# One load for w_down, fewer pieces at the end, and an output row cast in two halves: a cached attention block with a feed-forward block beside it, on one core

## The chip, the core and the metric

The kernel runs on one core of one Trainium2 chip. The metric is the device time of one execution in microseconds (us). The kernel before took 2534.58 us, the median of 3 runs (2534.54 to 2534.76). One further execution was profiled; it took 2534.51 us, of which the profile's span, from the first instruction to the last, covers 2532.6 us. All numbers taken from views of the profile belong to that execution.

## The reference

One token `x` (512 values) goes through two blocks, and a gate mixes the results.

```
g = sigmoid((x * gate_w).sum())
q = x @ wq                                  # 32 heads of 128
p = softmax(q . k_cache * 128 ** -0.5)      # 65536 keys for each head
a = (p @ v_cache) @ wo                      # wo is 4096 x 512
b = (silu(x @ w_gate) * (x @ w_up)) @ w_down   # 512 -> 1792 -> 512
out = g * a + (1 - g) * b                   # 512 values, bf16
```

`k_cache` and `v_cache` have the shape 1 x 32 x 65536 x 128 in bf16, 512 MB each. Every byte of them is used once, with a single query. `w_down` is 1792 x 512, 1.75 MB.

## The kernel before

**Tiles.** K and V come in tiles of 4 MB: 128 partitions, on each 128 cache rows of 128 values, so 32 KB that lie together in DRAM. There are N = 128 tiles of each, four to a head (`G`). All large tiles share one pool, `ring`, of five buffers of 4 MB: wq, the K and V tiles, the gate and up weights (`gu_t`), w_down (`wd_t`), and the last 16 heads of wo (`wo_t`).

**Scores.** `products` (L230) lets VectorE multiply a K tile by the query, in place (L240), and fold 128 columns to 16 by three additions of halves (L244). `scores` (L249) sums the 16 columns on TensorE into `S_ps`. After a head's four tiles `row_max` and `exponentials` (L263, L273) form the weights, with a maximum over all partitions taken through TensorE.

**Values.** `values` (L296) runs 32 matmuls for a V tile (L302), each with four cache rows of each partition, into a 4 x 512 accumulator `O_ps`, so that a head's result lies on the four diagonal blocks. `head_copy` (L311) brings it to SBUF on ScalarE; for the last head ScalarE takes one half and VectorE the other. `head_column` (L320) turns the four blocks into a column with eight small TensorE passes into `oh_ps`, and ScalarE scales it into `oT`. `project` (L334) adds the head's product with wo to the row `a_ps`. Heads 0 to 15 are projected as they come; heads 16 to 31 (`WH` = 16) only at the very end, when `wo_t` has been loaded.

**The order of work** is written out by hand: the pools run under a manual schedule, and the list `steps` (L344) says for each step which K tile and which V tile are treated. V starts four tiles behind K and is held back to eight tiles behind; after the last K tile, eight V tiles remain. In each step the loads are issued first, all of them from SyncE and so on one DMA queue, in the order in which they stand in the code. A load waits for its buffer to come free. It also waits for its completion semaphore: SyncE's loads go around eight of them, so a load waits until the one eight before it has landed. SyncE takes its instructions in order, so one load that waits holds those behind it.

**w_down before.** It is laid on 64 partitions, 28 rows of 512 on each (28 KB). `load_wd` (L142) loads it in eight transfers of eight partitions (L146): two before the third K tile (L150), six after it (L359). To fit that layout `feed_forward_mid` (L189) brings the hidden vector from 128 x 14 to 64 x 28 by two matmuls (L202) and a copy on ScalarE (L206), then runs 28 matmuls (L209) into `b_ps`.

**The end before.** The last V tile comes in five pieces, of 32, 32, 32, 16 and 16 of the 128 cache rows of each partition (L365); behind it come the last 16 heads of wo in five pieces of 4, 4, 4, 2 and 2 heads (L157, L366). After the last matmul of `values` the code projects heads 16 to 19, then forms the last head's column, then projects heads 20 to 31 (L405 to L410). VectorE casts the row of 512 (L413), and SyncE stores it (L414).

Of the kernel before, what the change touches and what calls it, by code (L numbers as in the profile page):

```python
# [8 lines left out]
ACT = mybir.ActivationFunctionType  # L9
ALU = mybir.AluOpType  # L10
AXIS = mybir.AxisListType
P = 128
# [3 lines left out]
NB = 128  # L16
# [9 lines left out]
def kernel(  # L26
# [14 lines left out]
    nc = tc.nc  # L41
    bf16 = mybir.dt.bfloat16
    f32 = mybir.dt.float32

    _, H, Sk, Dh = A_k_cache.shape
    D = A_x.shape[2]
    F = B_w_gate.shape[1]
    KT = D // P
    FT = F // P
    G = Sk // (NB * P)  # L50
    NBH = Sk // P
    N = H * G
# [4 lines left out]
    consts = ctx.enter_context(tc.tile_pool(name="consts", bufs=1))  # L57
# [7 lines left out]
    psum_m = ctx.enter_context(tc.tile_pool(name="psum_m", bufs=2, space=bass.MemoryType.PSUM))  # L65
# [3 lines left out]
    def big(name):  # L69
        return ring.tile([P, NB * Dh], bf16, name=name, tag="big")  # L70
# [12 lines left out]
    ident_b = consts.tile([P, P], bf16, name="ident_b")  # L83
# [14 lines left out]
    a_ps = psum_a.tile([1, D], f32, name="a_ps")  # L98

    K_tiles, V_tiles, S_tiles, P_tiles, O_tiles = {}, {}, {}, {}, {}  # L100

    def load(dst, cache, n, name, cuts=(0, NB)):
        h, g = divmod(n, G)
        t = big(name)
        view = t.rearrange("p (j d) -> p j d", d=Dh)
        src = cache[0, h, g * NB * P : (g + 1) * NB * P, :].rearrange("(p j) d -> p j d", j=NB)
        for a, b in zip(cuts[:-1], cuts[1:]):
            nc.sync.dma_start(out=view[:, a:b, :], in_=src[:, a:b, :])
        dst[n] = view
# [24 lines left out]
    nc.sync.dma_start(out=wgu_sb[:, 0], in_=B_w_gate.rearrange("(p t) f -> p t f", t=KT))  # L134
    nc.sync.dma_start(out=wgu_sb[:, 1], in_=B_w_up.rearrange("(p t) f -> p t f", t=KT))
    wd_t = big("wd_t")
    HP = P // 2
    GT = F // HP
    wd_sb = wd_t[:HP, : GT * D].rearrange("p (t n) -> p t n", t=GT)
    wd_rows = B_w_down.rearrange("(p t) n -> p t n", t=GT)  # L140

    def load_wd(*which):  # L142
        for i in which:
            lo = (0, 1, 2, 3, 32, 33, 34, 35)[i]
            part = slice(lo, lo + 29, 4)
            nc.sync.dma_start(out=wd_sb[part], in_=wd_rows[part])  # L146

    with nc.allow_non_contiguous_dma(reason="small"):
        nc.sync.dma_start(out=gwT, in_=gate_w.rearrange("(p t) -> p t", t=KT))
    load_wd(0, 1)  # L150
    WG = 4
    wo_tiles = {}

    WH = H // 2
    wo_end = []

    def load_wo_end(cuts):  # L157
        t = big("wo_t")[:, : (H - WH) * D].rearrange("p (h n) -> p h n", n=D)
        rows = A_wo[WH * P :, :].rearrange("(h p) n -> p h n", p=P)
        for a, b in zip(cuts[:-1], cuts[1:]):  # L160
            nc.sync.dma_start(out=t[:, a:b, :], in_=rows[:, a:b, :])
        wo_end.append(t)

    def load_wo(g):
        wo_tiles[g] = wo_pool.tile([P, WG, D], bf16, name="wo_sb")
        rows = A_wo[g * WG * P : (g + 1) * WG * P, :]
        nc.sync.dma_start(out=wo_tiles[g], in_=rows.rearrange("(h p) n -> p h n", p=P))
# [21 lines left out]
    def feed_forward_mid(gu_sb, eg):  # L189
        nc.vector.tensor_scalar_add(eg, eg, 1.0)  # L190
        nc.vector.reciprocal(eg, eg)
        hprod = consts.tile([P, FT], f32, name="hprod")
        nc.vector.tensor_tensor(out=hprod, in0=gu_sb[:, :FT], in1=eg, op=ALU.mult)
        hT = consts.tile([P, FT], bf16, name="hT")
        nc.vector.tensor_tensor(out=hT, in0=hprod, in1=gu_sb[:, FT:], op=ALU.mult)
        xg = consts.tile([P, KT], f32, name="xg")
        nc.vector.tensor_tensor(out=xg, in0=xT, in1=gwT, op=ALU.mult)
        xs = consts.tile([P, 1], f32, name="xs")
        nc.vector.tensor_reduce(out=xs, in_=xg, axis=AXIS.X, op=ALU.add)
        h_ps = psum_m.tile([HP, GT], f32, name="h_ps", tag="misc")  # L200
        for r in range(2):
            nc.tensor.matmul(  # L202
                h_ps[:, r * FT : (r + 1) * FT], lhsT=ident_b[:, r::2], rhs=hT, start=True, stop=True
            )
        h2 = consts.tile([HP, GT], bf16, name="h2")
        nc.scalar.activation(out=h2, in_=h_ps, func=ACT.Copy)  # L206
        b_ps = psum_m.tile([1, D], f32, name="b_ps", tag="misc")
        for t in range(GT):
            nc.tensor.matmul(  # L209
                b_ps, lhsT=h2[:, t : t + 1], rhs=wd_sb[:, t, :], start=(t == 0), stop=(t == GT - 1)  # L210
            )
        g_ps = psum_m.tile([P, 1], f32, name="g_ps", tag="misc")
        nc.tensor.matmul(g_ps, lhsT=ones_f, rhs=xs, start=True, stop=True)
        eg2 = consts.tile([P, 1], f32, name="eg2")
        nc.scalar.activation(out=eg2, in_=g_ps, func=ACT.Exp, scale=-1.0)
        return b_ps, eg2
# [13 lines left out]
    def products(n, a=0, b=NB):  # L230

        h = n // G
        K = K_tiles[n][:, a:b, :]
        qb = q_bc[:, h * Dh : (h + 1) * Dh]
        q_rep = bass.AP(
            tensor=qb.tensor,
            offset=qb.offset,
            ap=[list(qb.ap[0]), [0, b - a], [1, Dh]],
        )
        yield nc.vector.tensor_tensor(out=K, in0=K, in1=q_rep, op=ALU.mult)  # L240
        half = Dh
        while half > WIDTH:
            half //= 2
            yield nc.vector.tensor_tensor(  # L244
                out=K[:, :, 0:half], in0=K[:, :, 0:half], in1=K[:, :, half : 2 * half],
                op=ALU.add,
            )
# [43 lines left out]
    def weight(h, tot_ps):  # L291
        recip = small.tile([P, 1], f32, name="recip")
        nc.vector.reciprocal(recip, tot_ps)  # L293
        nc.vector.tensor_tensor(out=rg[:, h : h + 1], in0=recip, in1=gval, op=ALU.mult)
# [39 lines left out]
    def project(h):  # L334
        nc.tensor.matmul(  # L335
            a_ps,
            lhsT=oT[:, h : h + 1],
            rhs=wo_tiles[h // WG][:, h % WG, :] if h < WH else wo_end[0][:, h - WH, :],
            start=False,
            stop=(h == H - 1),  # L340
        )
# [3 lines left out]
    v = 0  # L345
# [9 lines left out]
    for n, v in steps:  # L355
        if n is not None and n > 1:
            load(K_tiles, A_k_cache, n, "K_t")
        if n == 2:
            load_wd(2, 3, 4, 5, 6, 7)  # L359
        if n == 3:  # L360
            load_wo(0)
        if v is not None:
            if v % (WG * G) == 2 * G and v // (WG * G) + 1 < WH // WG:
                load_wo(v // (WG * G) + 1)
            load(V_tiles, A_v_cache, v, "V_t", (0, NB) if v < N - 2 else (0, 64, NB) if v < N - 1 else (0, 32, 64, 96, 112, NB))  # L365
            if v == N - 1:  # L366
                load_wo_end((0, 4, 8, 12, 14, 16))
        if n == 2:
            ff = feed_forward_mid(*ff)
        halves = (0, NB // 2)  # L370
        vector = iter(()) if n is None else products(n)
        if n == 0:
            vector = (i for a in halves for i in products(n, a, a + NB // 2))
        top_of = None
        if n is None:
            top_of = H - 1 if S_tiles else None
        elif n % G == 0 and n > 0:
            top_of = n // G - 1
            vector = (i for a in halves for i in products(n, a, a + NB // 2))
        if top_of is not None:  # L380
            next(vector, None)
            mT_ps = row_max(top_of)
            next(vector, None)
            exponentials(top_of, mT_ps)
        for _ in vector:
            pass
        if n == 1:
            ff = feed_forward_in()
        if n == 3:
            feed_forward_out(*ff)  # L390
        if tot_ps is not None:
            weight(*tot_ps)
            tot_ps = None
        if done is not None:
            head_column(done, head_copy(done))
        if v is not None:
            values(v)
        if top_of is not None:
            tot_ps = top_of, total(top_of)
        if n is not None:  # L400
            scores(n)
        if done is not None and done < WH:
            project(done)
        done = v // G if v is not None and v % G == G - 1 else None
    O_last = head_copy(H - 1, last=True)  # L405
    for h in range(WH, WH + 4):
        project(h)
    head_column(H - 1, O_last)
    for h in range(WH + 4, H):
        project(h)  # L410

    out_sb = consts.tile([1, D], bf16, name="out_sb")
    nc.vector.tensor_copy(out=out_sb, in_=a_ps)  # L413
    nc.sync.dma_start(out=out[0], in_=out_sb)  # L414


# [28 lines left out]
```

## Time and profile before

| What | Value | Where it is read |
|---|---|---|
| profiled execution | 2534.51 us | times |
| its span | 2532.6 us | head of the page |
| three other runs | median 2534.58 us, 2534.54 to 2534.76 | times |
| bytes read from DRAM | 1087.64 MB, 429 GB/s over the span | page, part 3 |
| VectorE busy | 2175.5 us, 86% of the span | page, part 1 |
| TensorE matmuls busy | 1742.4 us, 69% | page, part 1 |
| share of the end's chain: DMA, PE, DVE | 68%, 22%, 10% | page, part 4 |
| matmul of `values`, 128 x 512 | 4096 of 453 ns busy | page, part 5 |
| matmul with w_down, 64 x 512 | 28, 12.1 us busy in all | page, part 5 |
| wo's last heads, pieces of 512 KB and 256 KB | 3 and 2 | view of the DMA issues, last 83 us |

PE is TensorE, PEld its weight loads, DVE is VectorE, ACT is ScalarE, SP is SyncE (SPq its DMA issues). The chain of part 4 is followed back from the last instruction, at each step to whatever released it. A group's line gives its source line, engine, operation, output and input, then busy time, mean length and the idle time ahead of it with what ended it. Matmuls overlap, so a group's busy time is more than the time by which it moves the end. The stage views give, for a stretch of time, each engine's busy time, then the granted TensorE clock (1.00 is full speed), then the mean busy share of the 16 DMA engines and their rate.

### The profile page before, as it was taken

Reading aid. Unit: us, or ns where it says so; the run is one execution under the profiler, and the core shown is the slowest. Engines: PE = TensorE matmul, PEld = TensorE weight load, DVE = VectorE, ACT = ScalarE, POOL = GpSimd, SP = SyncE. Lnnn points to the kernel's source line nnn. Section 1 sums busy time; section 2 is a strip of 40 time slices with the busy share of each in tenths; the row PEclk is TensorE's granted clock in tenths of the full one; section 3 lists DMA queues with packets and bytes.
Section 4 is the critical chain, followed back from the end, with each engine's and each line's share of the span. In section 5 each row is a group of like instructions: output and inputs, shape, how many; then the busy total and the mean of one; then the engine's idle time right before and its main releaser. Section 6 shows DMA issues by size and latency. Waiting matters only on the chain.

```text
span 2532.6 us, 15260 instructions
## 1 busy us (share of the span) xinstructions
PE 1742.4 (69%) x6738; PEld 712.1 (28%) x6738; DVE 2175.5 (86%) x784; ACT 75.9 (3%) x207; POOL 0.7 (0%) x6
## 2 busy tenths in 40 slices
PE   4677666776677666676776677667666776677679
PEld 2222222222222222222222223222222232222223
DVE  7998888888888999998888888888888888888860
ACT  1000000000000000000000000000000000000000
POOL 0000000000000000000000000000000000000000
PEclk7677777777777676677777777777777777777779
DMA  9999999999999999999999999999999999999998
GB/s 415 433 433 430 433 433 433 432 430 435 432 432 434 431 433 432 432 433 433 432 434 433 432 434 433 432 432 434 432 431 434 433 430 434 434 431 433 434 432 339
DMA packets 42884, 1088.63 MB, mean 430 GB/s; under 512 B 4737, under 2 KB 8834, under 8 KB 9090
## 3 DMA queue, kind: packets, MB, share of 16 engines
q1 hardware_dynamic: 42674, 1087.66, 99.7%
q8 instruction: 53, 0.87, 0.1%
q14 instruction: 13, 0.11, 0.0%
q10 hardware_dynamic: 144, 0.00, 0.0%
HBM read 1087.64 MB, written 0.00 MB: 429 GB/s over the span
## 4 chain that ended last, share of the span: by engine, by line
DMA 68%; PE 22%; DVE 10%; issue 1%; ACT 0%; DVEq 0%; SPq 0%
DMA V_t<-in_A_v_cache_dram 61%; PE O_ps L302 20%; DMA K_t<-in_A_k_cache_dram 5%; DVE K_t L240 5%; DVE K_t L244 5%; PE S_ps L254 1%; DMA wo_t<-in_A_wo_dram 1%; DMA wq_t<-in_A_wq_dram 0%; PE qg_ps L117 0%; DVE m L266 0%; PE oh_ps L323 0%; PE a_ps L335 0%; PE a_ps L227 0%; ACT P_sb L279 0%; DVE top L275 0%
## 5 line engine op out<-in xcount | busy, mean ns | idle before, releaser
L302 PE MATMUL O_ps<-V_t,P_sb 128*4 128x512 bf16 x4096 | 1157.3, 453 | 496.8 <-DMA V_t<-in_A_v_cache_dram 494.3
L240 DVE TENSOR_TENSOR K_t<-K_t,q_bc 128x16384 bf16<-128x16384 bf16 (+1 forms) x160 | 1117.2, 6983 | 254.4 <-DMA K_t<-in_A_k_cache_dram 232.9
L244 DVE TENSOR_TENSOR K_t<-K_t 128x4096 bf16<-128x4096 bf16 (+3 forms) x480 | 1030.9, 2148 | 14.3
L302 PEld LDWEIGHTS <-P_sb 128*4 128x4 bf16 x4096 | 393.9, 97 | 1241.0 <-issue 897.5
L254 PE MATMUL S_ps<-K_t,ident_b 128*128 128x128 bf16 x2048 | 466.0, 394 | 107.0 <-DVE K_t L244 106.9
L254 PEld LDWEIGHTS <-ident_b 128*128 128x128 bf16 x2048 | 227.6, 115 | 330.0 <-issue 140.2
L323 PE MATMUL oh_ps<-ident_f,O_sb 4*128 4x1 f32 x256 | 57.9, 343 | 74.1 <-ACT O_sb L315 74.1
L323 PEld LDWEIGHTS oh_ps<-ident_f,O_sb 4*128 4x128 f32 x256 | 55.2, 314 | 83.7 <-ACT O_sb L315 78.9
L270 PE MATMUL mT_ps<-diag,ones_f 128*128 128x128 f32 x64 | 23.6, 468 | 79.8 <-ACT diag L268 79.8
L268 ACT ACTIVATE diag<-ident_f,m 128x128 f32<-128x128 f32 x32 | 12.8, 401 | 2099.3 <-DVE m L266 2099.3
L317 DVE COPY O_sb<-O_ps 4x256 f32<-4x256 f32 x1 | 0.4, 414 | 52.1 <-ACT O_sb L315 52.1
L270 PEld LDWEIGHTS mT_ps<-diag,ones_f 128*128 128x128 f32 x64 | 14.7, 285 | 95.6 <-ACT diag L268 95.6
L266 DVE TENSOR_REDUCE m<-S_ps 128x1 f32<-128x512 f32 x32 | 21.9, 683 | 7.4 <-PE S_ps L254 7.4
L315 ACT ACTIVATE O_sb<-O_ps 4x512 f32<-4x512 f32 (+1 forms) x32 | 18.1, 566 | 131.0 <-PE O_ps L302 131.0
L279 ACT ACTIVATE P_sb<-S_ps,bias 128x512 bf16<-128x512 f32 x32 | 22.0, 687 | 1.0
L117 PE MATMUL qg_ps<-wq_t,X_bc 128*128 128x512 bf16 x32 | 8.6, 436 | 13.2 <-DMA wq_t<-in_A_wq_dram 13.2
L293 DVE RECIPROCAL recip<-tot_ps 128x1 f32<-128x1 f32 x32 | 5.1, 160 | 12.2 <-PE tot_ps L288 12.2
L209 PE MATMUL b_ps<-wd_t,h 64*1 64x512 bf16 x28 | 12.1, 629 | 4.3 <-DMA K_t<-in_A_k_cache_dram 4.3
L288 PEld LDWEIGHTS tot_ps<-rowsum,ones_f 128*128 128x128 f32 x64 | 9.5, 188 | 14.0 <-issue 14.0
L288 PE MATMUL tot_ps<-rowsum,ones_f 128*128 128x1 f32 x64 | 12.2, 260 | 0.0
L330 ACT ACTIVATE oT<-oh_ps,rg 128x1 bf16<-128x1 f32 x32 | 8.4, 263 | 76.6 <-PE oh_ps L323 76.6
L227 PE MATMUL a_ps<-b_sb,ones_f 1*1 1x512 f32 x2 | 1.9, 1032 | 12.1 <-ACT b_sb L226 12.1
(42 smaller groups left out, 73.8 us busy)
## 6 DMA issues: line engine op xcount, KB each, us to landing
K_t<-in_A_k_cache_dram SPq DMA_DIRECT2D x127, 4096.0 KB, 35.3
V_t<-in_A_v_cache_dram SPq DMA_DIRECT2D x126, 4096.0 KB, 29.1
wq_t<-in_A_wq_dram SPq DMA_DIRECT2D x1, 4096.0 KB
K_t<-in_A_k_cache_dram SPq DMA_DIRECT2D x2, 2048.0 KB, 16.8
V_t<-in_A_v_cache_dram SPq DMA_DIRECT2D x2, 2048.0 KB
V_t<-in_A_v_cache_dram SPq DMA_DIRECT2D x3, 1024.0 KB, 29.4
wo_sb<-in_A_wo_dram SPq DMA_DIRECT2D x4, 512.0 KB, 17.3
gu_t<-in_B_w_gate_dram SPq DMA_DIRECT2D x1, 1792.0 KB
```

What stands on the lines that cost most here:

```text
L209: nc.tensor.matmul(b_ps, lhsT=h2[:, t : t + 1], rhs=wd_sb[:, t, :], start=(t == 0), stop=(t == GT - 1))
L240: yield nc.vector.tensor_tensor(out=K, in0=K, in1=q_rep, op=ALU.mult)
L244: yield nc.vector.tensor_tensor(out=K[:, :, 0:half], in0=K[:, :, 0:half], in1=K[:, :, half : 2 * half], op=ALU.add,)
L254: nc.tensor.matmul(S_tiles[h][:, g * NB : (g + 1) * NB], lhsT=ident_b, rhs=K_tiles[n][:, :, c], start=(c == 0), stop=(c == WIDTH - 1),)
L266: nc.vector.tensor_reduce(out=m, in_=S_tiles[h], axis=AXIS.X, op=ALU.max)
L268: nc.scalar.activation(out=diag, in_=ident_f, func=ACT.Copy, scale=m)
L270: nc.tensor.matmul(mT_ps, lhsT=ones_f, rhs=diag, start=True, stop=True)
L279: nc.scalar.activation(out=P_tiles[h], in_=S_tiles[h], func=ACT.Exp, bias=bias, scale=scale, accum_out=rowsum[:, h : h + 1],)
L288: nc.tensor.matmul(tot_ps, lhsT=ones_f, rhs=rowsum[:, h : h + 1], start=True, stop=True)
L302: nc.tensor.matmul(O_tiles[h], lhsT=P_tiles[h][:, g * NB + j : g * NB + j + 4], rhs=V_tiles[n][:, j : j + 4, :], start=(g == 0 and j == 0) ...
L315: nc.scalar.activation(out=O_sb[:, :cut], in_=O_ps[:, :cut], func=ACT.Copy)
L323: nc.tensor.matmul(oh_ps, lhsT=O_sb[:, c * Dh : (c + 1) * Dh], rhs=ident_f[0:4, c : c + 1], start=(c == 0), stop=(c == 3),)
```

## The change

w_down is laid on all 128 partitions, 14 rows of 512 on each, and loaded by one transfer behind the third K tile. The conversion of the hidden vector goes, and 14 matmuls with 128 partitions take the place of 28 with 64. The last V tile comes in three pieces of 64, 48 and 16 cache rows of each partition, the last heads of wo in three pieces of 7, 6 and 3 heads. The last head's column is formed before all 16 remaining projections, instead of after four of them. The output row is cast by VectorE (left half) and ScalarE (right half).

```diff
     wd_t = big("wd_t")
-    HP = P // 2
-    GT = F // HP
-    wd_sb = wd_t[:HP, : GT * D].rearrange("p (t n) -> p t n", t=GT)
-    wd_rows = B_w_down.rearrange("(p t) n -> p t n", t=GT)
-
-    def load_wd(*which):
-        for i in which:
-            lo = (0, 1, 2, 3, 32, 33, 34, 35)[i]
-            part = slice(lo, lo + 29, 4)
-            nc.sync.dma_start(out=wd_sb[part], in_=wd_rows[part])
+    wd_sb = wd_t[:, : FT * D].rearrange("p (t n) -> p t n", t=FT)
...
-    load_wd(0, 1)
...
-        h_ps = psum_m.tile([HP, GT], f32, name="h_ps", tag="misc")
-        for r in range(2):
+        b_ps = psum_m.tile([1, D], f32, name="b_ps", tag="misc")
+        for ft in range(FT):
             nc.tensor.matmul(
-                h_ps[:, r * FT : (r + 1) * FT], lhsT=ident_b[:, r::2], rhs=hT, start=True, stop=True
-            )
-        h2 = consts.tile([HP, GT], bf16, name="h2")
-        nc.scalar.activation(out=h2, in_=h_ps, func=ACT.Copy)
-        b_ps = psum_m.tile([1, D], f32, name="b_ps", tag="misc")
-        for t in range(GT):
-            nc.tensor.matmul(
-                b_ps, lhsT=h2[:, t : t + 1], rhs=wd_sb[:, t, :], start=(t == 0), stop=(t == GT - 1)
+                b_ps,
+                lhsT=hT[:, ft : ft + 1],
+                rhs=wd_sb[:, ft, :],
+                start=(ft == 0),
+                stop=(ft == FT - 1),
             )
...
         if n == 2:
-            load_wd(2, 3, 4, 5, 6, 7)
+            nc.sync.dma_start(out=wd_sb, in_=B_w_down.rearrange("(p t) n -> p t n", t=FT))
...
-            load(V_tiles, A_v_cache, v, "V_t", (0, NB) if v < N - 2 else (0, 64, NB) if v < N - 1 else (0, 32, 64, 96, 112, NB))
+            load(V_tiles, A_v_cache, v, "V_t", (0, NB) if v < N - 2 else (0, 64, NB) if v < N - 1 else (0, 64, 112, NB))
             if v == N - 1:
-                load_wo_end((0, 4, 8, 12, 14, 16))
+                load_wo_end((0, 7, 13, 16))
...
     O_last = head_copy(H - 1, last=True)
-    for h in range(WH, WH + 4):
+    head_column(H - 1, O_last)
+    for h in range(WH, H):
         project(h)
-    head_column(H - 1, O_last)
-    for h in range(WH + 4, H):
-        project(h)
 
     out_sb = consts.tile([1, D], bf16, name="out_sb")
-    nc.vector.tensor_copy(out=out_sb, in_=a_ps)
+    nc.vector.tensor_copy(out=out_sb[:, : D // 2], in_=a_ps[:, : D // 2])
+    nc.scalar.activation(out=out_sb[:, D // 2 :], in_=a_ps[:, D // 2 :], func=ACT.Copy)
     nc.sync.dma_start(out=out[0], in_=out_sb)
```

## The prediction

> **What bounds the kernel now.** I read the page first, then the chain of waits at the end, the time line of the last 40 us, and the times at which the parts of each transfer land.
>
> ```profile
> DMA  9999999999999999999999999999999999999998
> ...
> L302 PE MATMUL O_ps<-V_t,P_sb 128*4 128x512 bf16 x4096 | 1157.3, 453 | 496.8 <-DMA V_t<-in_A_v_cache_dram 494.3
> L240 DVE TENSOR_TENSOR K_t<-K_t,q_bc 128x16384 bf16<-128x16384 bf16 (+1 forms) x160 | 1117.2, 6983 | 254.4 <-DMA K_t<-in_A_k_cache_dram 232.9
> ```
>
> The DMA engines are busy in every slice, and both compute engines idle because K or V has not landed (494.3 and 232.9 us). No edit changes the bytes, so only two things can move the time: when the last V tiles have landed, and what follows. The chain of the last 60 us:
>
> ```profile
> 2472.70 31.39 DMA V_t<-in_A_v_cache_dram
> ...
> 2504.16 20.87 DMA wo_t<-in_A_wo_dram
> 2525.03 0.04 issue
> 2525.07 1.02 PE a_ps L335 x4
> 2526.09 0.98 PE oh_ps L323 x8
> 2527.07 2.69 PE a_ps L335 x12
> 2529.76 0.02 issue
> 2529.79 0.68 DVE out_sb L413
> ```
>
> It names wo's load between 2504.16 and 2525.03. The time line shows that TensorE was busy through all of it:
>
> ```profile
> 2495.45 7.07 PE L302 MATMUL O_ps<-V_t,P_sb 128*4 128x512 bf16 x32
> 2504.14 20.88 PE L302 MATMUL O_ps<-V_t,P_sb 128*4 128x512 bf16 x96 [1.62 <-DMA V_t<-in_A_v_cache_dram]
> 2525.07 1.02 PE L335 MATMUL a_ps<-wo_t,oT 128*1 128x512 bf16 x4
> 2525.11 0.37 ACT L315 ACTIVATE O_sb<-O_ps 4x256 f32<-4x256 f32 x1 [29.29 <-PE O_ps L302]
> 2525.52 0.41 DVE L317 COPY O_sb<-O_ps 4x256 f32<-4x256 f32 x1 [52.13 <-ACT O_sb L315]
> 2526.02 1.05 PE L323 MATMUL oh_ps<-ident_f,O_sb 4*128 4x1 f32 x8
> ```
>
> So the end is: V's third-last tile lands at 2504.1, then 96 matmuls at 20.88/96 = 0.2175 us, then 0.98 + 2.69 us of PE behind the two copies, the cast, the store. The last piece of V landed at 2523.67, 1.3 us ahead of TensorE.
>
> Why did the tile land at 2504.1? The trace keeps, for each transfer, a landing for each of 16 DMA engines. Sorted, as us after the first of them:
>
> ```
> transfer (issued at)     first     the sixteen engines
> w_up (3.37)              40.49     0 .0 .1 .1 .1 .1 .2 .2 .3 .3 .3 .4 .4 .5 .6 .6
> 4th K tile (43.20)       60.10     0 .0 .0 .1 .3 .3 .4 .4 | 8.3 8.4 8.4 8.4 8.5 8.7 8.8 9.9
> 3rd-last V tile (2472.7) 2487.52   0 .0 6.7 6.7 6.8 6.8 7.0 7.3 7.8 8.4 8.4 8.5 9.1 12.7 15.5 16.6
> ```
>
> Each of the eight w_down transfers has only eight landings, and after them eight engines are 8.4 us behind: all eight transfers ran on the same eight engines. Later one engine at a time falls back 1.5 us, about every 49 us; the instruction queue (q8) has 53 transfers at that rhythm. Following the landings from tile to tile, these delays go around eight engines, six or seven each. Six of those had no w_down, two had it. Hence the last row: two engines with neither burden (0), six with delays alone (up to 8.5), six with w_down (one also has seven delays of 1.0: 12.7), and two with both (15.5, 16.6). A tile has landed when the last engine has.
>
> **The change part by part.** All against the profiled execution.
>
> *w_down in one load.* w_gate's and w_up's loads, of the same size on 128 partitions, landed 4.2 and 4.3 us after what was ahead of them (32.64, 36.85, 41.11 at the last engine), and all engines within 0.7. So each engine now gets 4.3: the two worst go from 16.6 and 15.5 to 12.5 and 11.4, the six with delays alone from 8.5 to 12.8. The last engine is then at 12.8: **V lands 3.8 us earlier**. Bounds: one instruction delay more or less on the last engine, ±1.5. The rest is hidden. On TensorE 14 matmuls of 12.1/28 = 0.43 us go (6 us), with two of 0.27 in all and a 0.19 us copy, all between 55 and 72 us, where the DMA share is 0.99 to 1.04; uncovered that would be a gain of 6.5. SyncE issues one load instead of eight. In the changed program the third K tile takes the buffer never used yet, and w_down wq's, free at 21.85. The engines reach w_down at 50.4, after the third K tile, and have it by 54.7 + 0.7, before its matmuls ran until now (60.35). The waits of the eight loads held the fourth K tile's issue to 43.20; it can go at 39.3, when its buffer is free. No load is issued later, and no DMA engine lacks work now.
>
> [...]
>
> *V's last tile in three pieces.* The second-last tile's halves landed at 2508.96 and 2513.82, so half a tile takes 4.9; five pieces landed at 2516.28, 2518.74, 2521.18, 2522.42, 2523.67. The pieces of 64, 48, 16 would land at 2518.7, 2522.4, 2523.7, and 3.8 earlier: 2514.9, 2518.6, 2519.9. TensorE starts the third-last tile at 2500.34 instead of 2504.14 (the whole run-up waits for the same late engines: 7.30 and 6.15 us at the V tiles before), and 64 matmuls end at 2514.26. Then 16 from 2514.95 to 2518.43, 12 from 2518.65 to 2521.26, 4 to 2522.13. That is 2.9 before 2525.02: of the 3.8, 0.9 go to the coarser pieces.
>
> *Four projections moved behind the column.* They now fill the 1.0 us in which TensorE waits for the copies. Behind the column they cost 4 x 0.2175 = **+0.87**. V's matmuls end at 2522.13; the copies and the column take 2.05 as now (2525.02 to 2527.07); 16 x 0.2175 = 3.48 and 0.08 for the last one's end follow, to 2527.74, against 2529.76 now.
>
> *wo's last heads in three pieces.* On the last engine 512 KB of wo took 1.36 us (2525.03, 2526.39, 2527.75), so 16 heads 5.44, behind V at 2519.9: pieces at 2522.3, 2524.3, 2525.3. They are wanted at 2524.2, 2525.7, 2527.0. Not on the path; uncovered it is 1.4 us away. With fewer pieces the semaphore waits end earlier (at V tiles landed by 2500.3).
>
> *The cast.* ScalarE's half waits for VectorE's in the changed program, as the two copies above do the other way round. Rows nearest: 0.41 (VectorE, 4x256) + 0.04 + 0.37 (ScalarE) = 0.82 for 0.68: **+0.14**. Bounds: -0.3 if they ran side by side, +0.4.
>
> [...] Side by side the sum below would be 0.4 lower.
>
> Sum: -3.8 + 0.9 + 0.87 + 0.14 = -1.9. 2534.51 - 1.9 = **2532.6 us**; the runs' median, 0.07 higher, gives 2532.7.
>
> **Rivals.**
>
> *Landings stay.* If something other than the late engines sets when V lands (the issue of the loads, say), only the losses remain: 0.9 + 0.87 + 0.14 = +1.9, **2536.4**. For it: SyncE waits long for TensorE's buffers. Against: the last three V tiles are issued 5 us and more before the engine that is furthest ahead has done with the load in front of them (2472.70 against 2477.79 for the first).
>
> *wo comes late.* Two of wo's issues took 3.73 and 5.62 us on SyncE, as if the queue were full, and the DMA share fell to 0.19:
>
> ```profile
> 2518.00:2520.00 2.00, 2.00 (x11) 0.80 (x10) 0.00 (x0) 0.00 (x0) 0.00 (x0) 1.00 0.45 172
> 2520.00:2522.00 2.00, 2.00 (x11) 0.77 (x9) 0.00 (x0) 0.00 (x0) 0.00 (x0) 1.00 0.19 75
> ```
>
> If larger pieces fill it again and the third lands where the last did (2529.11), the last three projections end at 2529.8, as now; with the cast **2534.7**. It decides from a landing after 2527.0. Against: the late engine still holds 4.4 us of wo when V is done.
>
> *The late engines are not w_down's.* Then spreading adds 4.3 us to the last engine: V's pieces land at 2523.0, 2526.7, 2528.0, V's matmuls end at 2530.2 instead of 2525.0, +5.2, and with 0.87 and 0.14 **2540.7**, slower. It decides if the engine at 16.6 comes from the group that had 0 at the 4th K tile. Against: those would need over ten delays of 1.5, and the instruction queue has 53 for eight engines.
>
> **How the numbers follow.** Forecast 2532.6: 0.72. wo late: 0.12. Landings stay: 0.10. Late engines elsewhere: 0.04. A gain over 0.2%, which would take more than is in the sum: 0.02. The range is 2531.0 to 2535.2: the forecast with one instruction delay fewer or more (2531.1, 2534.1) and wo late (2534.7), the cast's bounds on both; 0.16 is left out. 0.2%, about what a measurement of this kernel can tell from no change, is 5.1 us: faster 0.02, within 0.94, slower 0.04.
>
> **What would show it.** In the profile after: the sixteen landings of the fourth K tile within 2 us, those of the third-last V tile within 13 instead of 16.6, and its matmuls starting near 2500.3; TensorE waiting for V once or twice in the last 32; 16 projections in a row behind the column; ScalarE's cast behind VectorE's. I am wrong if the landings still spread by over 15 us, or if `a_ps` waits for wo.

## The result and the profile after

The changed kernel takes 2541.98 us (median of 8 runs, 2541.77 to 2542.20) against 2534.56 us for the kernel before (8 runs, 2533.17 to 2536.28). The ratio is 1.0031 with a 95% interval of 1.0021 to 1.0040: 7.4 us slower, where 1.9 us faster was forecast. The profiled execution took 2542.11 us, its span 2540.3 us.

The groups that wait for the caches, on the page of the changed kernel (busy time, mean, then idle time and what ended it):

```profile
DMA  9999999999999999999999999999999999999998
...
L289 PE MATMUL O_ps<-V_t,P_sb 128*4 128x512 bf16 x4096 | 1157.2, 452 | 510.7 <-DMA V_t<-in_A_v_cache_dram 508.3
L227 DVE TENSOR_TENSOR K_t<-K_t,q_bc 128x16384 bf16<-128x16384 bf16 (+1 forms) x160 | 1117.3, 6983 | 261.8 <-DMA K_t<-in_A_k_cache_dram 259.0
```

The busy times are the same to 0.2 us. The waits for V have grown from 494.3 to 508.3 us and those for K from 232.9 to 259.0, though the DMA engines are still full in every slice. The chain at the end:

```profile
2493.38 35.25 DMA V_t<-in_A_v_cache_dram
2528.63 0.04 issue
2528.67 3.63 PE O_ps L289 x16
...
2532.38 0.38 ACT O_sb L302
2532.76 0.04 issue
2532.80 1.05 PE oh_ps L310 x8
2533.85 3.56 PE a_ps L322 x16
2537.41 0.02 issue
2537.43 0.42 DVE out_sb L398
2537.86 0.02 issue
2537.88 0.37 ACT out_sb L399
```

It has the form that was forecast: the last 16 matmuls wait for a piece of V (here landed at 2528.63), then the copies, the column, 16 projections in a row, two casts one behind the other. It stands 10 us later than forecast (V's second piece was to land at 2518.6). The time line shows where this lateness is already complete:

```profile
2510.29 13.97 PE L289 MATMUL O_ps<-V_t,P_sb 128*4 128x512 bf16 x64 [1.69 <-DMA V_t<-in_A_v_cache_dram]
2524.97 7.32 PE L289 MATMUL O_ps<-V_t,P_sb 128*4 128x512 bf16 x32 [0.70 <-DMA V_t<-in_A_v_cache_dram]
```

The third-last V tile lets TensorE start at 2510.29; forecast was 2500.3. The landings on the sixteen DMA engines, as us after the first:

```
tile (changed kernel)       first     the sixteen engines                                           last
4th K tile                  64.64     0 to .4, one at 1.95                                          66.59
3rd-last V tile             2499.14   0 .0 .1 .2 .4 1.5 2.9 7.0 9.3 9.5 9.7 9.7 10.7 10.8 10.9 11.1 2510.25
the same in kernel before   2487.52   (shown ahead of the result)                           16.6    2504.09
```

So the evening-out did happen: the sixteen landings spread over 11.1 us instead of 16.6. But even the first of them now comes 11.6 us later than before. By the forecast at most 4.3 of that can be a share of w_down, so 7.3 us or more are lost even on the engine that is furthest ahead. Two more views show how. First the rate in the stage from 140 to 2400 us, where nothing was changed; the columns are the stretch, busy time of PE, PEld, DVE, ACT and POOL, the clock, the DMA share and GB/s. Before:

```profile
140.00:2400.00 2260.00, 1558.85 (x5914) 634.25 (x5914) 2006.32 (x712) 63.09 (x178) 0.00 (x0) 0.75 1.00 433
```

and after:

```profile
140.00:2400.00 2260.00, 1552.98 (x5889) 631.08 (x5889) 2002.43 (x711) 63.12 (x178) 0.00 (x0) 0.75 1.00 431
```

The DMA share is 1.00 in both, and the rate has fallen from 433 to 431 GB/s. Second, the trace's record of each packet. It holds 32512 packets of 32 KB, 128 for a tile; over sixteen engines that is 2032 on each in the mean:

```
32 KB packets       mean       most common lengths
before              1214.4 ns  1213 ns (99.5% of them)
after               1218.2 ns  1215 ns (50%), 1222 (20%), 1214 (9%), 1213 (6%)
```

3.8 ns on 2032 packets are 7.7 us on each engine, spread over the whole run. The same bytes from the same caches take longer to move.

**The theory** that I formed from this (A): the destination has moved. The copy that the change drops wrote a tile `h2` of 56 bytes for each partition, allotted 64. All that is allotted behind it moved down by 64 bytes, the five 4 MB buffers among it. In the allocation of the built programs they start at byte 30976 of a partition before, a multiple of 256, and at byte 30912 after, a multiple of 64 only. The rivals: (B) the one-piece load of w_down and the new order of the buffers slow the loads; (C) the chip, or the place of the caches in DRAM.

### The profile page after: what moved, and what is told of

It is laid out like the page before. It is cut to its first block, busy times and chain, and to the rows that moved or that the text cites. A ratio compares the mean times of both kernels' runs of the same rounds, so it can differ in the third digit from the quotient of the medians.

```text
span 2540.3 us, 15212 instructions
## 1 busy us (share of the span) xinstructions
PE 1735.5 (68%) x6722; PEld 709.2 (28%) x6722; DVE 2175.1 (86%) x784; ACT 76.1 (3%) x207; POOL 0.7 (0%) x6
## 4 chain that ended last, share of the span: by engine, by line
DMA 68%; PE 23%; DVE 8%; issue 1%; ACT 0%; SPq 0%; DVEq 0%; ACTq 0%
DMA V_t<-in_A_v_cache_dram 63%; PE O_ps L289 21%; DMA K_t<-in_A_k_cache_dram 5%; DVE K_t L227 4%; DVE K_t L231 4%; PE S_ps L241 1%; PE oh_ps L310 0%; DVE m L253 0%; PE a_ps L322 0%; PE a_ps L214 0%; ACT P_sb L266 0%; ACT O_sb L302 0%; PE mT_ps L257 0%; DVE top L262 0%; ACT diag L255 0%
## 5 line engine op out<-in xcount | busy, mean ns | idle before, releaser
L289 PE MATMUL O_ps<-V_t,P_sb 128*4 128x512 bf16 x4096 | 1157.2, 452 | 510.7 <-DMA V_t<-in_A_v_cache_dram 508.3
L227 DVE TENSOR_TENSOR K_t<-K_t,q_bc 128x16384 bf16<-128x16384 bf16 (+1 forms) x160 | 1117.3, 6983 | 261.8 <-DMA K_t<-in_A_k_cache_dram 259.0
L262 DVE TENSOR_REDUCE top<-mT_ps 128x1 f32<-128x128 f32 x32 | 9.0, 282 | 1.0 <-PE mT_ps L257 1.0
```

The source lines that it names most:

```text
L289: nc.tensor.matmul(O_tiles[h], lhsT=P_tiles[h][:, g * NB + j : g * NB + j + 4], rhs=V_tiles[n][:, j : j + 4, :], start=(g == 0 and j == 0) ...
```

## The experiments

**The changed kernel with its buffers put back.** One unused tile stands where `h2` stood; the buffers start at 30976 again.

```diff
+        pad = consts.tile([P, 28], bf16, name="pad")
+        nc.gpsimd.memset(pad, 0.0)
         b_ps = psum_m.tile([1, D], f32, name="b_ps", tag="misc")
```

> The changed kernel with a tile of 56 bytes per partition put where the removed one (h2) stood, so that the five 4 MB buffers start at byte 30976 of each partition again, a multiple of 256, instead of 30912 (a multiple of 64). Nothing else differs. Theory A, the place of the buffers: the 32 KB packets take 1213 ns again instead of 1215 to 1222, the third-last V tile lands at about 2500 instead of 2510, and the time is 2532 to 2533 us. Theory B, the single w_down transfer and the new order of the buffers (third K tile in the buffer never used, w_down in wq's): packets stay at 1215 to 1222 ns and the time near 2542. Theory C, the chip or where the caches lie in DRAM: as B, or packets that differ between kernels run on the same chip for no reason in their text.

Measured: 2531.93 us (2531.79 to 2532.42), ratio to before 0.9992 (0.9983 to 1.0000). 99.5% of the packets take 1213 ns again, mean 1214.2. The third-last V tile's last landing is at 2500.25, its spread 10.3 us. The rate in the middle is back at 433 GB/s:

```profile
140.00:2400.00 2260.00, 1559.26 (x5920) 634.70 (x5920) 2009.31 (x712) 63.05 (x178) 0.00 (x0) 0.75 1.00 433
```

One tile that nothing reads is worth 10 us. B falls: every edit of the change is in this kernel, the new order of the buffers too, and its packets are as short as before. The next run bears on C. The chain at the end is the forecast's, to within 0.7 us:

```profile
2484.34 33.98 DMA V_t<-in_A_v_cache_dram
2518.32 0.04 issue
2518.36 3.63 PE O_ps L291 x16
...
2522.07 0.38 ACT O_sb L304
2522.45 0.04 issue
2522.49 1.05 PE oh_ps L312 x8
2523.54 3.56 PE a_ps L324 x16
```

V's second piece landed at 2518.32 (forecast 2518.6), V's last matmul ended at 2521.99 (forecast 2522.13), and the last projection at 2527.10 (forecast 2527.74).

**The kernel before with its buffers moved**, by 192 bytes, so that they stand to 256 as in the changed kernel:

```diff
         h2 = consts.tile([HP, GT], bf16, name="h2")
+        pad = consts.tile([P, 96], bf16, name="pad")
+        nc.gpsimd.memset(pad, 0.0)
```

> The kernel before with one more tile of 192 bytes per partition, so that the five buffers start at byte 31168, 192 past a multiple of 256 as in the changed kernel. w_down, the end and the cast stay as before. Theory A: packets of 1215 to 1222 ns, mean near 1218, about 3.8 ns on each of some 2030 packets of an engine, so 7.5 to 8 us: 2542 us. Theory B and C: 1213 ns, 2534.6 us.

Measured: 2545.12 us (2543.67 to 2545.91), ratio 1.0040 (1.0026 to 1.0054). Packets: mean 1218.3 ns, 1215 ns for 50% and 1222 for 20%, as in the changed kernel. The sixteen landings of the third-last V tile spread by 16.4 us, as in the kernel before, and the last is at 2514.55. So the place alone makes the kernel before 10.6 us slower, where 7.5 to 8 were expected, and C falls too: the kernel before, run beside it on the same chip, took 2534.55. 8.0 of the 10.6 are in the 32 KB packets (3.96 ns x 2032). Of the rest, 2.5 us, the trace shows a part: the other data packets together grew by 0.6 us per engine, and the packets of the instruction queue (16 KB) grew from 929 to 1065 ns in the mean, which is 0.95 us on an engine that takes seven of them. About 1 us stays open.

```profile
140.00:2400.00 2260.00, 1543.58 (x5876) 627.74 (x5874) 1998.89 (x709) 63.06 (x178) 0.00 (x0) 0.75 1.00 431
```

The rate in the middle is 431 GB/s, as in the changed kernel.

**Which place, and whose.** Four more versions of the kernel before, each with only an unused tile added behind `h2`: `[P, 96]` with a gap of 64 bytes behind the five buffers, so that all smaller tiles behind them stand to 256 as before; `[P, 64]`; `[P, 16]`; `[P, 128]`.

```diff
+    behind = ctx.enter_context(tc.tile_pool(name="behind", bufs=1))
     small = ctx.enter_context(tc.tile_pool(name="small", bufs=2))
...
+    gap = behind.tile([P, 32], bf16, name="gap")
+    nc.gpsimd.memset(gap, 0.0)
```

> The kernel before with the five 4 MB buffers at byte 31168 (192 past a multiple of 256) and a gap of 64 bytes behind them, so that the small tiles, the weights P and wo's first heads stand where they stood against 256. If the place of the buffers themselves is what counts: packets 1215 to 1222 ns, third-last V tile's last landing near 2514, 2543 to 2546 us as in the second run. If the place of the other tiles did it (the engines' operands, the accumulators' copies): 1213 ns and 2534.6.

> The kernel before with all buffers 128 bytes further, at byte 31104, a multiple of 128 and not of 256. If packets need a multiple of 256: above 1213 ns and 2541 to 2546 us. If a multiple of 128 is enough: 1213 ns and 2534.6.

> The kernel before with all buffers 32 bytes further, at byte 31008, a multiple of 32 alone. If all places off a multiple of 256 cost the same, one extra part for each 32 KB packet: about 1218 ns in the mean and 2542 to 2546 us. If the cost grows as the place gets less even: clearly above 1218 ns and above 2546 us.

> The kernel before with all buffers 256 bytes further, at byte 31232, a multiple of 512 where the kernel before has a multiple of 256 only. If 256 is the whole rule: 1213 ns and 2534.6 us, no change. If a multiple of 512 is better still: under 1213 ns, and 2 us faster for each ns. It also tells that moving the buffers as such costs nothing.

Measured, with the two kernels and the run above:

```
buffers start at            past 256   32 KB packets, mean   time (ratio to before, 95%)
30976 (before)              0          1214.4 ns             2534.6
31232                       0          1214.3 ns             2534.61 (1.0001, 0.9992 to 1.0010)
31104                       128        1218.4 ns             2542.95 (1.0037, 1.0023 to 1.0050)
31168                       192        1218.3 ns             2545.12 (1.0040, 1.0026 to 1.0054)
31168, small tiles not      192        1218.0 ns             2544.30 (1.0038, 1.0023 to 1.0053)
31008                       32         1219.3 ns             2546.58 (1.0047, 1.0031 to 1.0064)
```

Moving the buffers by 256 costs nothing (2534.61 us), and this place, a multiple of 512, is no better than the one before, a multiple of 256 only (1214.3 and 1214.4 ns). 128 bytes past a multiple is not enough (1218.4 ns). 32 past is dearest in the packets, by 1 ns; the times of the four moved versions overlap in their intervals, so whether the cost grows as the place gets less even is not decided. It is the large buffers that count: with the small tiles behind them left in place against 256 the cost is the same (1218.0 ns, 2544.30 us; its third-last V tile landed at 2512.06, where 2514 was expected).

**The two halves of the change**, each with the buffers at 30976. First the end alone, in the kernel before (three pieces of V and of wo, the column first, two casts; the edits are those of the diff above):

```diff
-            load(V_tiles, A_v_cache, v, "V_t", (0, NB) if v < N - 2 else (0, 64, NB) if v < N - 1 else (0, 32, 64, 96, 112, NB))
+            load(V_tiles, A_v_cache, v, "V_t", (0, NB) if v < N - 2 else (0, 64, NB) if v < N - 1 else (0, 64, 112, NB))
...
-                load_wo_end((0, 4, 8, 12, 14, 16))
+                load_wo_end((0, 7, 13, 16))
...
-    for h in range(WH, WH + 4):
+    head_column(H - 1, O_last)
+    for h in range(WH, H):
         project(h)
```

> The kernel before with only the edits at the end: V's last tile and wo's last heads in three pieces, the column ahead of all 16 projections, the cast by two engines. Buffers at byte 30976. All theories: landings of V as before (third-last tile at 2504.1), then 0.9 for the coarser pieces, 0.4 for the order (the changed kernel shows 5.11 us from V's last matmul to the last projection against 4.74) and 0.15 for the cast: about 2536.0.

Measured: 2535.81 us (2534.42 to 2536.67), ratio 1.0003 (0.9994 to 1.0012). The interval takes in no change as well as the 1.4 us expected: inconclusive by itself. The trace of its profiled execution says more. From the last landing of the third-last V tile to the issue of the store it is 27.90 us (2503.16 to 2531.06), against 26.40 in the kernel before (2504.09 to 2530.49): the new end costs 1.5 us. That the tile landed 0.9 us earlier in this one execution hid a part of it.

Then w_down alone: the changed kernel's w_down with the end of the kernel before.

```diff
+        pad = consts.tile([P, 28], bf16, name="pad")
+        nc.gpsimd.memset(pad, 0.0)
...
-                load_wo_end((0, 7, 13, 16))
+                load_wo_end((0, 4, 8, 12, 14, 16))
...
-    head_column(H - 1, O_last)
-    for h in range(WH, H):
+    for h in range(WH, WH + 4):
+        project(h)
+    head_column(H - 1, O_last)
+    for h in range(WH + 4, H):
         project(h)
```

(V's five pieces and the single cast are put back in the same way.)

> The changed kernel's w_down (one transfer on 128 partitions) with the end of the kernel before, and the buffers held at byte 30976 by a tile of 56 bytes. Theory A: the sixteen landings of the third-last V tile spread by 11 to 13 us instead of 16.6, its last one is near 2500.3, and the time is 2530.5 to 2531.5. Theory B: packets above 1213 ns and about 2540. A third view, that the spread of the landings has no part in the end: 2534.6.

Measured: **2530.47 us** (2530.36 to 2530.62), ratio 0.9985 (0.9976 to 0.9993): faster than both kernels. Third-last V tile: spread 10.4 us (11 to 13 were expected), last landing 2500.38. Its end:

```profile
2468.79 31.59 DMA V_t<-in_A_v_cache_dram
2500.38 0.04 issue
2500.42 20.88 PE O_ps L291 x96
2521.30 0.99 PE a_ps L324 x4
2522.29 0.98 PE oh_ps L312 x8
2523.27 2.69 PE a_ps L324 x12
```

These are the steps of the kernel before (whose chain gave the 96 matmuls' time to wo's load), 3.7 to 3.8 us earlier. This run and the one with the buffers put back differ in the end alone: 2531.93 - 2530.47 = 1.5 us is what the new end costs.

## Why the prediction was wrong, step by step

**The step that failed** is the sentence "The rest is hidden" under w_down. It listed the dropped copy as 0.19 us of ScalarE behind DMA and asked no more of it. With the copy went the tile it wrote, and with the tile the place of the buffers. The premise "No edit changes the bytes, so only two things can move the time" failed in the same place. The landing of the last V tiles did move, but the prediction looked for its causes in the bytes and in their spread over the engines alone. It took the length of a packet as given (99.5% took 1213 ns in the kernel before), and an edit in the allocation ahead of the buffers changed it (1218.2 ns in the mean after, 1214.4 before). The term missing from the sum is 2541.98 - 2531.93 = +10.05 us. Summed over all its packets, an engine's time is 9.5 us longer in the changed kernel than in the same kernel with its buffers put back (2537.0 against 2527.5 us in the mean), 8.1 of that in the 32 KB packets. Neither of the two signs by which the prediction would have known itself wrong appeared: the landings spread by 11.1 us, and `a_ps` did not wait for wo.

**Landings 3.8 us earlier: right.** With the buffers put back the last landing of the third-last V tile moved from 2504.09 to 2500.25. The forecast put the last engine 12.8 us behind the old first one, at 2487.52 + 12.8 = 2500.3. The first landing came 2.5 us later (2489.98). That fits the forecast's own figures for an engine that had carried w_down, 6.7 - 8.4 + 4.3 = 2.6, though the trace does not name the engines; so the spread is 10.3. Against this run the landings of the changed kernel are 9.2 us later at the first engine and 10.0 at the last.

**Coarser pieces of V, +0.9: right.** From the first matmul of the third-last tile to V's last it is 21.70 us with three pieces (2500.29 to 2521.99) and 20.88 with five: +0.82.

**The order of column and projections, +0.87: too dear.** From V's last matmul to the last projection it is 5.11 us with the column first (2521.99 to 2527.10) and 4.66 with four projections first (2521.30 to 2525.96): +0.45. I took the time to the column (1.0 us) from the kernel before, where the four projections themselves filled it. The column needs ScalarE's half first, and starts 0.50 us after V's last matmul when nothing stands ahead of it; in the run with the buffers put back VectorE's copy ends after the column has begun.

**The cast, +0.14: right as far as it shows.** The two halves run one after the other, 0.41 and 0.37 us, and the store is issued 0.85 us after the cast's start (2527.12 to 2527.97) instead of 0.70 (2525.99 to 2526.69): +0.15.

**wo in three pieces, nothing: right.** In the changed kernel they landed at 2532.43, 2534.58 and 2535.62; the 16 projections started at 2533.85 and ran without a gap (3.56 us). The third piece was issued at 2523.70, late, as that rival feared (the second had held SyncE for 23.1 us), and was still in time.

**The rivals.** "Landings stay" falls with the landings. "The late engines are not w_down's" gave 2540.7 us, near the measured time, by a mechanism that was not there: the spread shrank, where by this rival it would not have. A number that fits is no evidence; its landings tell it apart.

With its four terms as measured the forecast would have been -3.8 + 0.8 + 0.45 + 0.15 = -2.4, so 2532.1 for the profiled execution; the run with the buffers put back gave 2531.83 in its profiled execution.

Two smaller things in the prediction are off and change none of this. From the terms that it names the range would run from 2530.7 to 2535.0, not from 2531.0 to 2535.2. Each w_down transfer has nine landing records, not eight: one comes 1.0 to 1.2 us after the issue, and the other eight 14 us or more after that one.

## What to carry to other kernels

When a kernel is bound by DMA at a share of 1.00, look at the length of its packets as well as at their number, and compare the allocation of the two programs before costing an edit at nothing: here a tile of 56 bytes that went moved every buffer behind it, and with it came packets of 1218.2 ns in the mean instead of 1214.2, and 10.05 us. It is worth trying the large DMA buffers at a multiple of 256 bytes of a partition, for instance by padding as in these runs: the two such places tried here gave 1214.4 and 1214.3 ns, the places 32, 128 and 192 past one 1218.0 to 1219.3. And TensorE took up the third-last V tile only when the last of its sixteen landings was there (2504.09, first matmul 2504.14, in the kernel before), so bytes spread over all sixteen engines can end earlier than bytes put on eight of them: for w_down that was worth 3.7 us at this tile (2504.09 to 2500.38 with w_down's edit alone).

## What the runs showed of the hardware

- **Packets of 32 KB into SBUF** took 1214.4 and 1214.3 ns in the mean with the buffers at bytes 30976 and 31232, both multiples of 256 (1213 ns for 99.5% of them at 30976), and 1218.0 to 1219.3 ns at places 32, 128 and 192 past one: 0.3 to 0.4% more. 32 past was the dearest, at 1219.3 ns. Why a moved packet takes longer was not shown; only the place in SBUF was changed.
- **Instruction loading fell on eight of the sixteen DMA engines**, as the landings show it; the trace does not name the engines. With the buffers put back, eight engines stand 8.5 to 10.3 us behind the first at the third-last V tile, and the instruction queue had 52 transfers of 16 KB, six or seven for each of the eight. By these numbers one transfer puts its engine back by about 1.4 us, an estimate: 0.93 us for its own packet, and 0.48 us by which a 32 KB packet that overlaps it in time takes longer than 1213 ns. In the changed kernel it is about 1.55 us (1.07 and 0.48), and eight engines stand 9.3 to 11.1 us behind. So this skew is about as large as what the place of the buffers is worth (10.05 us), and the last landing sets the end: with the buffers put back it is at 2500.25, and the tile's first matmul at 2500.29. The instruction packets took 928 to 936 ns in the mean in all five kernels with buffers at a multiple of 256, and 1065 to 1074 in the five others, though they load no tile; why is not shown.
- **The eight transfers of w_down, eight partitions each, all ran on the same eight engines**: after them eight landings of the fourth K tile lie within 0.4 us and the other eight 8.3 to 9.9 us later. In 28 KB packets of 1062 ns, one for each of the eight transfers, that is 8.5 us.
